# Attention beside a gated GLU on one core: the values' PSUM bank released after each run of value matmuls, queries split into two parts when they are made, and a new order of the work

## The chip, the cores and the metric

One core of one Trainium2 chip runs the whole kernel. The metric is the device time of one launch in microseconds, the median of several runs. The kernel before has a median of 1625.59 us over three runs (1625.26 to 1625.67).

## The reference

With S = 2048 rows, D = 512, H = 32 heads of width 16, one shared head of keys and values, and F = 1792, all in fp32:

```python
q = (x @ wq).reshape(B, S, H, Dh).transpose(0, 2, 1, 3)
k, v = x @ wk, x @ wv                                   # one head, width 16
p = softmax(einsum("bhqd,bkd->bhqk", q, k) * Dh ** -0.5)
a = einsum("bhqk,bkd->bhqd", p, v) -> (B, S, 512) @ wo
b = (sigmoid(x @ w_gate) * (x @ w_up)) @ w_down
g = sigmoid((x * gate_w).sum(-1, keepdims=True))
out = g * a + (1 - g) * b
```

## The kernel before

**Numbers split in two.** The matrix products that need fp32 accuracy run as products of two rounded parts. A tile is rounded to the matmul's own type (the high part), and what the rounding lost is kept as a second tile (the low part); `split` (line 706) does both, and a product takes three matmuls.

**Units of attention.** A unit is one block of 512 query rows for one group of four heads: 4 blocks times 8 groups are 32 units. The queries of a unit lie in a tile `qs` of 128 partitions by 2 by 512. Its upper and lower 64 partitions each hold, for one head parity, 16 rows of the high part, the same 16 rows again, 16 rows of the low part, and in the last two rows the negated row maxima; the key tile `ks` is stacked to match, so one matmul over 64 partitions gives a score block less its maximum. There are three `qs` tiles, used in turn.

A unit goes through these steps. `query` (line 901) makes queries of two units on TensorE, `query_out` (904) copies them out of PSUM on ScalarE, `store_q` (908) sends them to DRAM. `load_q` (919) brings them back with six DMAs into the tile `stage`, and `stack` (926) makes the parts of `qs` from it on GpSimd (a cast of the whole tile and two subtractions over 16 partitions; for unit 0 on ScalarE and VectorE). `maximum` (1062) forms scores without the maxima, 64 matmuls, each followed by a VectorE reduction that reads its PSUM bank. `max_turn` (940) transposes the maxima on TensorE, and `send_max` writes them into `qs`. `scores` (1071) forms 64 score blocks, and ScalarE's exponential takes each from PSUM into a tile `p` (22 buffers). `pv`, line 955 (the matmuls carry line 958), multiplies the exponentials of 128 keys by the values: 16 steps to a unit, each of four matmuls 32 columns wide that lie side by side on the array (eight records in the trace), all 16 adding into one PSUM bank. A column of ones beside the values gives the softmax sums. `finish` (963) copies that bank out on ScalarE, and `store`, `sums`, `invert`, `send_inverse`, `spread` and `divide` do the division.

**The GLU beside it.** `fill` (1035) issues the matmuls of gate, up, down and output projections, each on 64 of the 128 partitions. `h_split`, `w_split` and `add_part` are GpSimd's share of it.

**The order of everything.** The class `State` holds a plan of the core: clocks of each engine, when each of the 8 PSUM banks is free, when buffers and DMAs are done. The string `ORDER` is the list of TensorE's steps, found by a search beforehand, and `plan()` walks it. One character is one step. A hexadecimal digit is a step in the two halves of the array: its two upper bits say what the first 64 partitions do and the two lower bits what the other 64 do (1 a maximum, 2 a score block, 3 a GLU matmul, 0 nothing). `V` is a value step on all 128 partitions, `T` a transpose of maxima, `G` a projection of queries or keys or a turn of the values, `.` a short time in which TensorE is given nothing. All work of the other engines is placed by the plan between these steps: what depends on a step is put on its engine's queue behind it, and GpSimd's tasks are picked by rank when their inputs should be there. At the end of the program, each engine's instructions are chained in exactly this order. A wrong guess of the plan costs a wait and nothing else.

In the order before, a value step may stand anywhere; the unit's bank (`self.sum`) is taken at its first value step and given back after its 16th (`issue_v`):

```python
        if c == 0:
            self.sum = self.take()
        self.acts.append(("values", u, c, self.sum))
...
        if c == NC - 1 and u < NU - 1:
            self.acts.append(("finish", u, self.sum))
```

Of the kernel before, what the change touches and what calls it, by code (L numbers as in the profile page):

```python
# [9 lines left out]
F32 = mybir.dt.float32  # L10
# [8 lines left out]
P = 128  # L19
# [11 lines left out]
RAW, WB, DB, PB, HB, BA_BUFS = 2, 2, 4, 22, 6, 4  # L31
# [11 lines left out]
RED, GATED, SUM, ENDS, PARTS, INVERSE = 260, 258, 285, 60, 225, 70  # L43
# [67 lines left out]
class State:  # L111

    def __init__(self):
# [27 lines left out]
        self.loaded, self.stage_free, self.unit_ready, self.max_ready, self.q_ready = 0, 0, {}, {}, {}  # L141
# [52 lines left out]
    def may(self, t):  # L194
        what, u, *_ = t[3]
        if what == "h" and self.slot_of("hl") is None or what == "divide" and self.slot_of("o") is None:
            return False
        if what == "stack" and (min(self.mp) < (u - 1) * NC * 2 or min(self.ep) < (u - 2) * NC * 2):
            return False
        return t[2] <= self.now  # L200

    def run(self, t):
        self.tasks.remove(t)
        what, *args = t[3]
        if what == "w":
            wide = args[0][0] in "gu"
            cost = (not self.early(args[0])) * CAST_W + TWO_W if wide else (1 + (args[0][0] != "e")) * (CAST + TWO)
        else:
            cost = {"h": CAST + TWO, "add": TWO, "stack": CAST_W + 2 * TWO_W, "divide": CAST + 2 * TWO, "x": 2 * TWO,
                    "xf": 4 * TWO, "wq": TWO}[what]  # L210
# [13 lines left out]
        elif what == "stack":  # L224
            self.stage_free, self.unit_ready[args[0]] = at, at + SURE
# [45 lines left out]
    def event(self, what, args):  # L271
# [3 lines left out]
        elif what == "store_q":  # L275
            at = self.send(1, 256)
            self.q_ready[tuple(args)] = at
            self.ba_release(("query", *args), at)
        elif what == "stack":
            self.stage_free = self.unit_ready[args[0]] = self.on("dve", self.on("act", self.now, 2 * COPY), 4 * RED)  # L280
# [8 lines left out]
        elif what == "store":  # L289
            self.after(self.send(5, 136) + SAFE, "sums", *args)  # L290
# [164 lines left out]
    def load_next(self):  # L455
        u = self.loaded
        if u < NU and self.stage_free <= self.now and self.q_ready.get((u // NG, u % NG // 2), NEVER) <= self.now:
            self.acts.append(("load_q", u))
            self.stage_free = NEVER
            self.loaded += 1  # L460
            at = self.send(6, 384)
            if u == 0:
                self.after(at, "stack", u)
            else:
                self.task(0, at, "stack", u)
# [35 lines left out]
    def can_v(self):  # L501
        return (self.first > GROUPS.index(("turn", NB - 1, 0)) and self.vp < NU * NC and bool(self.exps)
                and (self.vp % NC > 0 or min(self.free) <= self.now)
                and self.exps[0][0] == 4 and self.exps[0][1] <= self.now)

    def issue_v(self):
        u, c = divmod(self.vp, NC)
        if c == 0:
            self.sum = self.take()
        self.acts.append(("values", u, c, self.sum))  # L510
# [5 lines left out]
        if c == NC - 1 and u < NU - 1:  # L516
            self.acts.append(("finish", u, self.sum))
            at = self.on("act", self.now + LATE, COPY) + TAIL_A
            self.free[self.sum] = at + FREE
            self.after(at, "store", u)  # L520
# [24 lines left out]
    def issue_g(self):  # L545
# [9 lines left out]
        else:  # L555
# [11 lines left out]
            else:  # L567
                at = self.on("act", at, COPY)
# [28 lines left out]
    def step(self, code):  # L597
# [10 lines left out]
        else:  # L608
            if self.full:
                self.now += OUT  # L610
# [11 lines left out]
    "GGGGGGGG555G555G5554GG5551G55G555GG5545G55G555G555GG555G555GT555Gd7fffd7bedbf7edbf7e9fe7fbde7bf9f6fedbf6fffd7bdf"  # L622
    "e7bf9f6fd7d7efVVVV96bfff9f7def6ffd7d7VVV96ffdf6ff9ff6fdbf7bdfe7fdbf6ffdb7dfef7V969V696V596VTVb9f7ff9f6ffdef6fdfb"
    "7edff6fbdf7bf9f7fed6.VV965VV96fdfb7eff96fbdf6fbdef6f9fb7edbf6fbde7fbd7eV969V696V969V696V969V696V956VVTbe9ff7ef9f"
    "e7bf9fe7ef9V695VV696Vb9fe7fedbf6fbdef6fbd7VVVdb6fbde7fbdeb7edbf7edffbf6fdbf6f9f7ebdef7VVV969V569VV697fff9f7efdef"
    "7bdV6bdeff6fbdbf6fbdef6fbdbf6VV969VT695VV6b9fff6fdebf6ff9f7df79VV6e9fff6fdbef6ff9f7d7VV96bffd7ef9fe7bde7bf9f7eed"
    "bf7f9ef6ff9f6fd7bdVVV695VV6bedff6fbdbf6fbdef6fbd7VVV9ebf7fedbf6fbdeffb5V696VT965VV95efffbf6bfdef6fbd7f9.VV6dbfef"
    "6fbd7fbde7ffdb6VVd6bfdb7ef9fe7bdef6f9fffb7efdbf6f9fe7bdef7VV969V696V596VV9eb7ff9fe7ef9fe7bf9f7d7VVVT9eeff7ef9fe7"
    "bf9fe7eV969V695VV6bdff7edbf7fedb7ff9f6ffdef6fdfb7bdf7d7dVVV79ef7edbf6f9fe7bdef6fbdb7efdb7ef9fe7bdef6fbV9a6V955VV"
    "696V9a6V969VTVV6fbdef6fbdbf6fd7df6VV9fb7fed7bfef9fe7bf9f7deV695VV6bedff6fbdbf6fd7df6VV96bffd7bf9fe7edbe7f9f7edbV"  # L630
    "V696V9e7bff9f7deV6bdfef7bd7eVV96fbff9f7ed.Ve6fdbf7bef9VTV6dbff7edbef7bf9f7edf6V965VVb9fe7fedbf6fbdef6fd7bVV96fdf"
    "f6fdbf7bfde7fd7VVd6fbdb7ef9fe7bdef6f9ffffb7edbf6f9f7ebdef7df6f9ff7d7bffdf7dfVV69aVV69aV696Va95V696VTV9eb7ff9fe7e"
    "f9fe7bf9fe7df6fbdVVV6fb9ff6fde7fbe.9.V696V965VVd6bfdb7ef9f6fdbe7bfdef6f9f7bedbf7ef9f6fd7d7VV965VVbdef6fbdbf6fbde"
    "f6fd7bVVV9ebf7fedbf6fbdef6fbdbVTV6bf9ff6fedbf6fdb7f9VVV69efff6fdb7f9ff6fedf7d7V9a6V965VV5bedfb7ef9f6fbde7bf9fffe"
    "7efd7fbedbf7edbf6..VV9651VVb6bfdfe7bf9fe7ef9fe7dVVV6bbdff6fbdefb7efdbe7dV696V969V569VTVb6fbdfe7bf9fe7ef9fe7dVV6b"
    "f9ff6fbdef6fbdf79f4dVV79fe7edbf6fbde7bf9f6ffffe9f7df6f9ff7edbfVV655VV969Ve6bfdfb7ef9fe7bf9fe7ef9f7d7VVVT9eeff7be"
    "df7bef9V696V965VV96dfff6ff9f7bfdebf7dfe7beff5f9fef7fbde7V969VVV6bdef7bdfe7bedb7ebf9f7efde7fbd6fbde7bf9f7deVV696V"
# [537 lines left out]
```

## Time and profile before

| | |
|---|---|
| median of three runs | 1625.59 us |
| span of the profiled execution, first to last instruction | 1623.6 us |
| TensorE matmul busy | 1615.1 us, 99% of the span, 12918 matmuls |
| VectorE busy | 1413.0 us, 87%, 2358 instructions |
| ScalarE busy | 1184.5 us, 73%, 2274 instructions |
| GpSimd busy | 774.2 us, 48%, 598 instructions |
| DMA | 98.09 MB, mean 60 GB/s |
| granted TensorE clock | 1.000 |

In the profile PE is TensorE's matmul and PEld its weight load, DVE is VectorE, ACT ScalarE, POOL GpSimd, SP the queue that issues the DMAs. In a timeline the first column is the start in us from the begin of the span, the second the length, and x8 the number of instructions merged into the row. A row of two matmuls on 64 partitions each that start together is one step of two halves. In a table of lines there stand the busy time, the mean ns of one instruction, and the idle time of the engine just before them with what ended it.

### The profile page before, as it was taken

What the parts mean: (1) busy time and instruction counts of PE and PEld (TensorE: products, weight loads), DVE (VectorE), ACT (ScalarE), POOL (GpSimd) and SP (SyncE); (2) the same over time, 40 slices, a digit from 0 to 9 for tenths busy, and PEclk for the clock granted to TensorE, in tenths of its full rate; (3) what the DMA queues carried; (4) which work ended last, traced back from release to release, by engine and by line L of the source; (5) the groups of instructions that cost most, each with busy time, mean ns of one, the idle gap of its engine ahead of it and who ended that gap; (6) DMA issues with size and microseconds to landing.
All of it is one profiled execution on the core that took longest, in us unless ns stands there. A gap on an engine that the chain in (4) does not pass through costs nothing.

```text
span 1623.6 us, 33417 instructions
## 1 busy us (share of the span) xinstructions
PE 1615.1 (99%) x12918; PEld 976.3 (60%) x12918; DVE 1413.0 (87%) x2358; ACT 1184.5 (73%) x2274; POOL 774.2 (48%) x598
## 2 busy tenths in 40 slices
PE   9999999999999999999999999999999999999998
PEld 7765566556566565655665556665566656565554
DVE  6999898989998998989889999988998988998842
ACT  4267777778777777777767777767877777787786
POOL 5354264356453535354735446435745453536253
PEclk9999999999999999999999999999999999999999
DMA  7411111024111212111411111102411121211011
GB/s 238 142 40 45 44 54 53 22 70 109 57 43 49 76 35 67 31 44 54 124 41 57 57 57 55 49 26 70 109 57 47 45 77 31 70 31 35 31 35 40
DMA packets 52371, 98.09 MB, mean 60 GB/s; under 512 B 17976, under 2 KB 19512, under 8 KB 51188
## 3 DMA queue, kind: packets, MB, share of 16 engines
q1 hardware_dynamic: 52212, 95.96, 19.2%
q8 instruction: 101, 1.65, 0.4%
q14 instruction: 58, 0.48, 0.1%
HBM read 74.05 MB, written 8.90 MB: 51 GB/s over the span
## 4 chain that ended last, share of the span: by engine, by line
PE 99%; ACT 0%; DVE 0%; issue 0%; DVEq 0%; POOL 0%; ACTq 0%; POOLq 0%
PE bank L1046 31%; PE bank L958 30%; PE bank L1067 18%; PE bank L1076 16%; PE bank L814 4%; PE bank L944 0%; ACT p L1078 0%; PE bank L836 0%; DVE ba L1123 0%; PE bank L884 0%; PE bank L1119 0%; ACT x L732 0%; ACT ba L1027 0%; DVE ba L1009 0%; DVEq L1171 0%
## 5 line engine op out<-in xcount | busy, mean ns | idle before, releaser
L1069 DVE TENSOR_REDUCE mx<-bank 128x1 f32<-128x512 f32 x2048 | 1285.4, 683 | 131.6 <-PE bank L1067 65.8
L1078 ACT ACTIVATE p<-bank 128x512 f32<-128x512 f32 x2048 | 1064.7, 618 | 331.7 <-PE bank L1076 171.2
L1076 PE MATMUL bank<-qs,ks 64*128 64x512 f32 x2048 | 743.5, 406 | 0.0
L1067 PE MATMUL bank<-ks,qs 62*128 62x512 f32 x2048 | 714.5, 410 | 0.5 <-ACT q L906 0.3
L958 PE MATMUL bank<-p,v_aug 128*32 128x512 f32 x4096 | 503.1, 600 | 0.0
L1076 PEld LDWEIGHTS bank<-qs,ks 64*128 64x128 f32 x2048 | 356.4, 185 | 136.7 <-DVE mx L1069 58.9
L1067 PEld LDWEIGHTS bank<-ks,qs 62*128 62x128 f32 x2048 | 343.5, 184 | 156.6 <-DVE mx L1069 55.1
L1046 PE MATMUL bank<-wd,hl 64*128 64x512 f32 x1344 | 261.8, 393 | 0.0
L958 PEld LDWEIGHTS bank<-p,v_aug 128*32 128x32 f32 x4096 | 101.8, 108 | 224.7 <-issue 199.2
L1046 PE MATMUL bank<-xs,wu 64*128 64x512 f32 x672 | 211.4, 392 | 0.0
L1046 PE MATMUL bank<-x,wu 64*128 64x512 f32 x672 | 210.1, 393 | 0.0
L1046 PE MATMUL bank<-xs,wg 64*128 64x512 f32 x672 | 210.0, 392 | 0.0
L1046 PE MATMUL bank<-x,wg 64*128 64x512 f32 x672 | 207.7, 392 | 0.0
L1046 PEld LDWEIGHTS bank<-wd,hl 64*128 64x128 f32 x1344 | 181.8, 185 | 27.6 <-issue 2.5
L932 POOL TENSOR_TENSOR qs<-stage,qs 16x1024 fp32r<-16x1024 f32 x62 | 148.7, 2398 | 4.8
L1046 PEld LDWEIGHTS bank<-x,wg 64*128 64x128 f32 x672 | 118.7, 185 | 11.2 <-POOL wu L790 0.8
L1046 PEld LDWEIGHTS bank<-x,wu 64*128 64x128 f32 x672 | 117.0, 185 | 12.0 <-issue 2.5
L1046 PEld LDWEIGHTS bank<-xs,wu 64*128 64x128 f32 x672 | 118.1, 186 | 9.2 <-issue 0.8
L1046 PEld LDWEIGHTS bank<-xs,wg 64*128 64x128 f32 x672 | 118.1, 186 | 8.8
L930 POOL CAST qs<-stage 128x1024 fp32r<-128x1024 f32 x31 | 32.3, 1041 | 158.0 <-PE bank L1076 101.2
L1030 POOL TENSOR_TENSOR ba<-ba,pa_d 128x512 f32<-128x512 f32 x48 | 61.9, 1291 | 91.8 <-DVE ba L1009 72.2
L789 POOL CAST wu<-ru 128x1024 fp32r<-128x1024 f32 x27 | 28.0, 1038 | 158.3 <-PE bank L1046 110.3
(85 smaller groups left out, 1064.4 us busy)
## 6 DMA issues: line engine op xcount, KB each, us to landing
rg<-wg SPq DMA_DIRECT2D x28, 512.0 KB
ru<-wu SPq DMA_DIRECT2D x28, 512.0 KB
rd<-wd SPq DMA_DIRECT2D x28, 512.0 KB
stage<-qd SPq DMA_DIRECT2D x192, 64.0 KB
xs<-x SPq DMA_DIRECT2D x16, 512.0 KB
xf<-x_in SPq DMA_DIRECT2D x16, 256.0 KB
qd<-q SPq DMA_DIRECT2D x16, 256.0 KB
ra<-wo SPq DMA_DIRECT2D x8, 512.0 KB
```

Source lines behind the costliest of these rows:

```text
L789: nc.gpsimd.tensor_copy(WS[item][:, 0, :], raw)
L814: nc.tensor.matmul(ps, w[:, p, part(kc)], X[b, kc][:, q, :], start=i == 0, stop=i == 3 * KC - 1)
L930: (nc.scalar.copy if u == 0 else e.tensor_copy)(qs, stage)
L932: e.tensor_tensor(qs[r], stage[r], f32(qs[r]), op=ALU.subtract)
L958: nc.tensor.matmul(ps[32 * j:32 * j + 32, :], v_aug[:, c, :], PT.pop((u, c, j)), start=c == 0, stop=c == NC - 1)
L1030: nc.gpsimd.tensor_tensor(BA[b, t], BA[b, t], PA.pop((b, t)), op=ALU.add)
L1046: nc.tensor.matmul(banks[i], l, r, start=at == 0, stop=at == j.n - 1)
L1067: nc.tensor.matmul(banks[i], qs_t[u % 3][r, pr, part(qt)], ks[r, kb * 512:(kb + 1) * 512], start=True, stop=True)
L1069: nc.vector.tensor_reduce(MX[u][:, pr, h, qt, kb:kb + 1], banks[i], axis=AX.X, op=ALU.max)
L1076: nc.tensor.matmul(banks[i], ks[r, part(c)], qs_t[u % 3][r, pr, :], start=True, stop=True)
L1078: nc.scalar.activation(p, banks[i], AF.Exp, scale=0.25)
```

## The change

Three things are changed, and the order is searched anew for them.

1. **The value bank.** A run of value steps now ends with the first two-half step behind it, or with the unit. `release` closes the accumulation there, and `finish` copies the bank out on ScalarE and gives it back. The first part of a unit goes to a tile `ou` (two buffers); each further part goes to a tile `vp` (two buffers), and `add_sums` adds it to `ou` on GpSimd. The next run takes a fresh bank. The last unit keeps one bank for all its runs.
2. **The queries.** `query_out` makes the two parts at once, ScalarE the high one and VectorE the low one, each its own `p` buffer; `store_q` sends both, two DMAs in place of one; `load_q` brings them straight into `qs`, six DMAs as before. `stack` and the tile `stage` are gone. The three `qs` tiles are zeroed once at the start, in place of `stage`.
3. **Buffers.** There are 21 `p` buffers in place of 22.

```diff
-RAW, WB, DB, PB, HB, BA_BUFS = 2, 2, 4, 22, 6, 4
+RAW, WB, DB, PB, HB, BA_BUFS = 2, 2, 4, 21, 6, 4
+OU, VB = 2, 2
...
     def issue_v(self):
         u, c = divmod(self.vp, NC)
-        if c == 0:
+        if self.sum is None:
             self.sum = self.take()
-        self.acts.append(("values", u, c, self.sum))
+        self.run_of.append(["values", u, c, not self.run_of, False, self.sum])
+        self.acts.append(self.run_of[-1])
...
+        if c == NC - 1:
+            self.release()
+
+    def release(self):
+
+        u, last = (self.vp - 1) // NC, self.vp % NC == 0
+        if u < NU - 1 or last:
+            self.run_of[-1][4] = True
+        if u == NU - 1:
+            return
+        self.run_of = []
+        if self.first_part:
...
+            self.acts.append(("finish", u, True, self.sum))
+            at = self.on("act", max(self.now + LATE, self.sums_free[i]), COPY)
...
+        else:
+            k = self.vp_free.index(min(self.vp_free))
+            assert self.vp_free[k] < NEVER
+            self.acts.append(("finish", u, False, self.sum))
+            at = self.on("act", max(self.now + LATE, self.vp_free[k]), COPY)
+            self.vp_free[k] = NEVER
+            self.task(0, at + SURE, "add_sums", u, last, k)
+        self.first_part = last
+        self.free[self.sum], self.sum = at + TAIL_A + FREE, None
...
         else:
             if self.full:
+                if self.sum is not None:
+                    self.release()
                 self.now += OUT
...
     def query_out(b, t, ps):
-        QD[b, t] = ap.tile([P, TB], F32, tag="p", name=f"q{b}_{t}", bufs=PB)
-        nc.scalar.copy(QD[b, t], ps)
+        hi, lo = QD[b, t] = [ap.tile([P, TB], F32R, tag="p", name=f"q{b}_{t}_{i}", bufs=PB) for i in range(2)]
+        nc.scalar.copy(hi, ps)
+        nc.vector.tensor_tensor(lo, ps, f32(hi), op=ALU.subtract)
...
-    def stack(u):
-
-        qs = qs_t[u % 3]
-        e = nc.vector if u == 0 else nc.gpsimd
-        (nc.scalar.copy if u == 0 else e.tensor_copy)(qs, stage)
-        for r in (slice(32, 48), slice(96, 112)):
-            e.tensor_tensor(qs[r], stage[r], f32(qs[r]), op=ALU.subtract)
+            for n, i in enumerate((0, 0, 1)):
+                r = 64 * par + n * DH
+                nc.sync.dma_start(qs[r:r + DH], qd[i, g % 2, par].rearrange("d pr t -> d (pr t)"))
...
-    def pv(u, c, ps):
+    def pv(u, c, start, stop, ps):
 
         for j in range(4):
-            nc.tensor.matmul(ps[32 * j:32 * j + 32, :], v_aug[:, c, :], PT.pop((u, c, j)),
-                             start=c == 0, stop=c == NC - 1)
...
+            nc.tensor.matmul(ps[32 * j:32 * j + 32, :], v_aug[:, c, :], PT.pop((u, c, j)), start=start, stop=stop)
...
+    def finish(u, whole, ps):
+
+        to = ap.tile([P, TB], F32, tag="ou" if whole else "vp", name=f"ou{u}", bufs=OU if whole else VB)
+        nc.scalar.copy(to, ps)
...
+    def add_sums(u, *_):
+        nc.gpsimd.tensor_tensor(SUMS[u], SUMS[u], PARTS_OF[u].pop(0), op=ALU.add)
```

`ORDER` is replaced as a whole. One line from its first tenth and its last line, before and after:

```diff
-    "bf7f9ef6ff9f6fd7bdVVV695VV6bedff6fbdbf6fbdef6fbd7VVV9ebf7fedbf6fbdeffb5V696VT965VV95efffbf6bfdef6fbd7f9.VV6dbfef"
...
-    "feVVaaVeec8V8ececV88cccccV"
+    "df6fddd7dVVVTV6ef7f6f9febdf6f9f6fbe7fbdf9e7fe7bf9dbf6ff5dVV695VV696V5bfef6f9fbdef6bdb7ff5dVV5a6.V969V7b6efdfe79f"
...
+    "Vaa8VV..............Vcccccccccccc"
```

Counted in the two strings. A stretch is what stands between two hexadecimal digits, made of `V`, `T`, `G` and `.` with at least one letter; a run holds value steps of one unit with nothing but `T` or `.` between them, and after the change each run of the units 0 to 30 is one part with a `finish` of its own.

| | before | after |
|---|---|---|
| value steps `V`, transposes `T`, projections and turns `G` | 512, 32, 24 | 512, 32, 24 |
| two-half steps, steps of one half | 4236, 28 | 4242, 16 |
| stretches, of them with a `V` | 307, 293 | 239, 224 |
| `T` with a `V` or `G` on both sides | 14 | 26 |
| runs of the units 0 to 30 | 282 | 232 |
| `.` | 10 | 23, of them 14 ahead of the last `V` |
| `c` behind the last `V` | 0 | 12 |

More of the change, by code (lines that the diff above doesn't have):

```diff
@@ L223, in run @@
             self.add_done(*args[1:], at)
-        elif what == "stack":
-            self.stage_free, self.unit_ready[args[0]] = at, at + SURE
+        elif what == "add_sums":
+            u, last, k = args
+            self.vp_free[k] = at
+            if last:
+                self.after(at, "store", u)
         elif what == "divide":
@@ L275, in event @@
         elif what == "store_q":
-            at = self.send(1, 256)
+            at = self.send(2, 512)
             self.q_ready[tuple(args)] = at
             self.ba_release(("query", *args), at)
-        elif what == "stack":
-            self.stage_free = self.unit_ready[args[0]] = self.on("dve", self.on("act", self.now, 2 * COPY), 4 * RED)
         elif what == "turn_x":
@@ L502, in can_v @@
         return (self.first > GROUPS.index(("turn", NB - 1, 0)) and self.vp < NU * NC and bool(self.exps)
-                and (self.vp % NC > 0 or min(self.free) <= self.now)
+                and (self.sum is not None or min(self.free) <= self.now)
                 and self.exps[0][0] == 4 and self.exps[0][1] <= self.now)
@@ L515, in issue_v @@
         self.vp += 1
[L516 to L520, printed above, removed]
+        if c == NC - 1:
[8 more added lines that the diff above has]
+        if self.first_part:
+            i = u % OU
+            assert self.sums_free[i] < NEVER
+            self.acts.append(("finish", u, True, self.sum))
+            at = self.on("act", max(self.now + LATE, self.sums_free[i]), COPY)
+            self.sums_free[i] = NEVER
+            if last:
+                self.after(at + TAIL_A, "store", u)
+        else:
[7 more added lines that the diff above has]
+        self.free[self.sum], self.sum = at + TAIL_A + FREE, None
     def can_t(self):
@@ L621 @@
 ORDER = (
[L622 to L626, printed above, removed]
@@ L632 @@
[L632 to L636, printed above, removed]
@@ L830, in tile_kernel @@
     nc.gpsimd.memset(v_aug, 1.0)
-    stage = cp.tile([P, 2, TB], F32, name="stage")
-    nc.gpsimd.memset(stage, 0.0)
+    qs_t = [cp.tile([P, 2, TB], F32R, name=f"qs{i}") for i in range(3)]
+    for i in range(3):
+        nc.gpsimd.memset(f32(qs_t[i]), 0.0)
     def early(n):
@@ L854, in tile_kernel @@
     gom = cp.tile([P, NC], F32, name="gom")
-    qs_t = [cp.tile([P, 2, TB], F32R, name=f"qs{i}") for i in range(3)]
     wq_s = []
```

118 lines of the change are left out of this document (62 added, 56 removed).

## The prediction

> **What bounds the kernel now.** I read the page's busy times first, then the busy times in three stretches, then the chain that ended last.
>
> ```profile
> span 1623.6 us, 33417 instructions
> PE 1615.1 (99%) x12918; PEld 976.3 (60%) x12918; DVE 1413.0 (87%) x2358; ACT 1184.5 (73%) x2274; POOL 774.2 (48%) x598
> 120.00:1600.00 1480.00, 1479.76 (x12113) 885.86 (x12107) 1304.75 (x2166) 1115.59 (x2148) 715.00 (x551) 1.00 0.18 54
> PE 99%; ACT 0%; DVE 0%; issue 0%; DVEq 0%; POOL 0%; ACTq 0%; POOLq 0%
> ```
>
> Between 120 and 1600 us TensorE lacks 0.24 us of being busy throughout, and the chain is TensorE from end to end. A busy TensorE may still be slow, though, since the rows say only that some matmul is in flight. So I look at how far apart its steps start, in a timeline of TensorE alone, ahead of and behind two runs of value steps (L958; x8 is one `V`, x24 three, x4 one cut by the window's end):
>
> ```profile
> 610.21 0.40 PE L1076 MATMUL bank<-qs,ks 64*128 64x512 f32 x1
> 610.45 0.39 PE L1046 MATMUL bank<-x,wg 64*128 64x512 f32 x1
> 610.78 1.07 PE L958 MATMUL bank<-p,v_aug 128*32 128x512 f32 x8
> 611.77 0.50 PE L1076 MATMUL bank<-qs,ks 64*128 64x512 f32 x1
> 612.12 0.63 PE L1076 MATMUL bank<-qs,ks 64*128 64x512 f32 x2
> 612.35 0.40 PE L1067 MATMUL bank<-ks,qs 62*128 62x512 f32 x1
> 612.68 2.78 PE L958 MATMUL bank<-p,v_aug 128*32 128x512 f32 x24
> 615.39 0.50 PE L1067 MATMUL bank<-ks,qs 62*128 62x512 f32 x1
> 615.74 0.39 PE L1046 MATMUL bank<-xs,wu 64*128 64x512 f32 x1
> 615.97 0.39 PE L1067 MATMUL bank<-ks,qs 62*128 62x512 f32 x1
> ```
>
> A two-half step takes 0.23 to 0.24 us (610.21 to 610.45, 615.74 to 615.97). The last one ahead of a value step takes 0.33 (610.45 to 610.78), 0.10 more. A lone value step takes 0.99 (610.78 to 611.77) and three take 2.71 (612.68 to 615.39), so a value step inside a run takes (2.71 - 0.99) / 2 = 0.86, and the last of a run 0.13 more. The first two-half step behind a run takes 0.35 (611.77 to 612.12; 615.39 to 615.74), 0.12 more. Going from two halves to the whole array and back thus costs 0.10 + 0.13 + 0.12 = 0.35 us by these rows, each good to 0.01 or 0.02. Behind the run quoted further down the first step takes 0.34 (1222.64 to 1222.98). I take 0.33 for the whole and keep 0.31 to 0.35.
>
> This makes the span up: 4236 two-half steps of 0.234 are 991 us, 512 value steps of 0.86 are 440, 307 stretches of 0.33 are 101; 92 of the 1623.6 us are left for 24 projections and turns, 32 transposes, the start and the end. Waiting adds little: in the table of waits (us in all, times, longest) the score blocks' weight loads wait for a reduction 71 times, never over 0.8 us.
>
> ```profile
> PEld bank L1076 <- DVE mx L1069: 58.9, 71, 0.8
> PEld bank L958 <- issue: 199.2, 630, 0.4
> PEld bank L958 <- ACT p L1078: 21.7, 59, 0.7
> ```
>
> (Most of these figures are the idle weight path between loads, which the matmuls cover.) So the time is the count of TensorE's steps times their durations, and a stretch fewer is worth 0.33 us, if nothing new waits.
>
> **The order.** The stretches go from 307 to 239: 68 x 0.33 = 22.4 us less. The two-half steps go up by 6 (+1.4 us), the one-half steps down by 12; of those the `c` at the end cost a full step and the others, of alternating halves, about half of one, so they give back about as much. Transposes move into the middle of runs:
>
> ```profile
> 1220.44 1.07 PE L958 MATMUL bank<-p,v_aug 128*32 128x512 f32 x8
> 1221.44 0.28 PE L944 MATMUL bank<-consts,mm 128*16 128x128 f32 x1
> 1221.64 1.06 PE L958 MATMUL bank<-p,v_aug 128*32 128x512 f32 x8
> 1222.64 0.49 PE L1076 MATMUL bank<-qs,ks 64*128 64x512 f32 x1
> 1222.98 0.40 PE L1076 MATMUL bank<-qs,ks 64*128 64x512 f32 x1
> ```
>
> The value step ahead of the transpose takes 1.00, not 0.86, and so does the one behind it, where the run ends: a `T` in the middle pays the way out of a value step once more, about 0.13. There are 26 - 14 = 12 more of them: +1.6 us. Left of the saving: 20.8 us.
>
> The Trainium skill, "TensorEngine Tiling (Array Packing)", Key Properties, says that changing the tiling mode drains TensorE. By that rule a transpose between value steps is a change on each side and would cost two drains; at a whole 0.33 us each of the 12 the saving would be 18.4 us. The rows show only the one 0.13, and the sum goes by them.
>
> **The fresh bank of each run.** After the change each of 232 runs opens a bank that an exponential or a reduction has just left, where now 31 units do. The weight loads of value steps that waited for an exponential idled 21.7 / 59 = 0.37 us each, those that waited for nothing visible 199.2 / 630 = 0.32. The difference, 0.05, times 201 more openings is 10 us; but the bank is also one more to choose from, so below it the bound is nothing. The timeline gives a nearer price: the first and the last of the 31 openings that follow a two-half step are
>
> ```profile
> 92.43 0.39 PE L1046 MATMUL bank<-x,wu 64*128 64x512 f32 x1
> 92.77 0.64 PE L958 MATMUL bank<-p,v_aug 128*32 128x512 f32 x4
> 1535.73 0.39 PE L1046 MATMUL bank<-xs,wu 64*128 64x512 f32 x1
> 1536.06 1.06 PE L958 MATMUL bank<-p,v_aug 128*32 128x512 f32 x8
> ```
>
> and all 31 start 0.359 us behind the step ahead on the average, the 262 other run starts 0.341. I take the 0.018 between them, 3.6 us.
>
> **ScalarE's copies, GpSimd's sums, the queries.** These lie beside TensorE.
>
> ```profile
> L966 ACT COPY ou<-bank 128x512 f32<-128x512 f32 x31 | 18.3, 591 | 40.2 <-PE bank L958 40.2
> L1078 ACT ACTIVATE p<-bank 128x512 f32<-128x512 f32 x2048 | 1064.7, 618 | 331.7 <-PE bank L1076 171.2 <-PE bank L1067 120.6 <-PE bank L1046 31.6
> L1030 POOL TENSOR_TENSOR ba<-ba,pa_d 128x512 f32<-128x512 f32 x48 | 61.9, 1291 | 91.8 <-DVE ba L1009 72.2 <-ACT pa_d L1027 12.0 <-ACT p L1078 3.8
> L932 POOL TENSOR_TENSOR qs<-stage,qs 16x1024 fp32r<-16x1024 f32 x62 | 148.7, 2398 | 4.8
> L930 POOL CAST qs<-stage 128x1024 fp32r<-128x1024 f32 x31 | 32.3, 1041 | 158.0 <-PE bank L1076 101.2 <-PE bank L1067 51.1 <-PE bank L1046 5.7
> L738 POOL TENSOR_TENSOR x<-xf,x 128x512 fp32r<-128x512 f32 x8 | 10.1, 1292 | 12.0 <-ACT x L732 12.0
> L738 DVE TENSOR_TENSOR x<-xf,x 128x512 fp32r<-128x512 f32 x8 | 6.5, 847 | 4.3 <-ACT x L732 4.3
> L877 DVE SCALAR_TENSOR_TENSOR ks<-kh,consts,bank 128x512 fp32r<-128x512 f32 x4 | 3.0, 748 | 3.2 <-ACT kh L876 3.0
> ```
>
> ScalarE gets 232 - 31 = 201 copies of 0.59 us, 119 us: from 1184.5 to 1303, 81% of about 1607. The 331.7 us that it idles ahead of exponentials covers them. Behind each copy are queued the exponentials of the next score blocks, for whose `p` the next run waits; the copy delays them by 0.59 us, which the 21 buffered `p` (five value steps) hide. Without that cover a run would start up to 0.59 later.
>
> GpSimd loses 148.7 + 32.3 = 181 us of stacking and gets 201 additions of 1.29 us, 259 us, and two more zeroings: 774 to some 855 us, 53%. Behind an addition are queued the splits of weights and hidden rows; for the addition itself waits the `vp` buffer, for that the second next `finish`, and behind that on ScalarE all exponentials. I cost this at nothing while the two buffers hold; the rival below prices it.
>
> The Trainium skill, "GPSIMD Engine Reference", 4.1 Engine selection, speaks against this choice: a two-input elementwise operation belongs on VectorE, GpSimd being about half as fast. Here the same 128x512 subtraction takes 1292 ns on one and 847 on the other, a factor of 1.5. By the rule the 201 additions would go to VectorE, and at 847 ns they would bring its 1423 us (below) to 1593, 99% of the new span, and it would then be the bound; by the rows GpSimd has the room.
>
> VectorE gets 16 subtractions out of PSUM. The nearest row is 748 ns: +12 us, all in the first 100 us, less two of unit 0's stack; 1423 us, 89%. Bounds: nothing, if they fall beside the projections (12 matmuls, some 2.8 us of TensorE, for each), to 10 us, if the first maxima wait for them; I take nothing, since VectorE was busy for 44 of the first 60 us.
>
> ```profile
> 0.00:60.00 60.00, 58.35 (x268) 43.17 (x269) 44.03 (x78) 26.48 (x43) 34.06 (x27) 1.00 0.71 224
> qd<-q SPq DMA_DIRECT2D x16, 256.0 KB
> stage<-qd SPq DMA_DIRECT2D x192, 64.0 KB
> ```
>
> The queue SP gets 16 more stores of 256 KB, 4.2 MB; at the 224 GB/s of these 60 us that is 19 us of transfer, in a stretch where the engines are 71% busy. Only unit 0 waits for its own, and loses its stack (a 1.05 us cast and two subtractions); I cost it at nothing, with 2 us either way. For all later units the load is issued about when the stack ran before, and the 1.04 + 2 x 2.40 us of stacking fall away ahead of the first maximum; TensorE did not wait there, so this gains nothing.
>
> **The end.** Fourteen `.` stand ahead of the last value step and the last 12 GLU matmuls behind it.
>
> ```profile
> 1611.32 1.31 PE L1046 MATMUL bank<-we,o 64*128 64x512 f32 x5
> 1612.56 1.06 PE L958 MATMUL bank<-p,v_aug 128*32 128x512 f32 x8
> 1614.12 0.71 PE L1105 MATMUL bank<-consts,ou_last 128*128 128x128 f32 x4 [0.49 <-ACT ou_last L1103]
> ```
>
> A one-half step costs 0.23 here ((1.31 - 0.39) / 4 for five). Twelve take 2.8 us behind the last value step, in which the copy hides that TensorE waits for now (0.49); before, ten of them stood ahead of it. The wait for the last exponentials and the additions behind the 12 cost between 0 and 2 us; I take 1.
>
> **The sum.** -20.8 + 3.6 + 1 = -16.2 us. The profiled span is 1623.6, so 1607.4; the median lies 2.0 us above the span, and I forecast **1609.4 us**. This case alone runs from 1601 (68 x 0.35, nothing for the banks and the end, 2 gained at the start) to 1621 (68 x 0.31, 10 lost at the banks, 2 at the end, some 3 at the start).
>
> **Rivals.** *The additions hold ScalarE up (slower).* Place: a unit's third and later parts. GpSimd works off its queue in order; a wide split is 1.04 + 2.39 us, two hidden rows 2 x 1.9. If it is in such work while two parts wait, the next `finish` has no `vp` buffer, ScalarE stands with the exponentials behind it, and TensorE stops at the next run. With runs 3 us apart, as between the short stretches, and 7.2 + 1.3 us ahead of the first free buffer, one such event costs some 2.5 us. Eight would bring the gain under 0.2%, twelve would give 1639 us. For it: GpSimd is at 53% and ScalarE has only this ring of two. Against it: the additions have first rank, and the waits quoted show that TensorE hardly ever stood for a task placed by the order. 8%.
>
> *ScalarE's copies eat the gain.* Its exponentials are late by part of each copy: 0.09 us in each of 201 parts costs 18 us, giving 1625 to 1628. For it: 81% busy and idle during long runs, so the rest must suffice. Against it: 300 us idle are left. 7%.
>
> *The stretches are not what costs.* If the 0.33 us is not paid for the change between forms but for something which stands at those places, say the weights' first load, it still stands there 68 times less. If it is a wait for exponentials, it moves into the longer runs and the time stays at 1622 to 1626. The nearly equal 0.33 and 0.35 at each run speak against a wait. 4%.
>
> **How the numbers follow.** The forecast's case has 81%. The range 1601 to 1622 holds it and the near edge of the two middle rivals. A measurement of this kernel can tell about 0.2% (3.3 us) from no change: faster has the 81% and a few points of the middle rivals, 0.85; no change 0.06; slower 0.09.
>
> **What would show it.** In the profile after: TensorE's steps still 0.234 us apart, 0.86 inside a run, 0.33 for each of 239 stretches; copies of value sums 232, additions 201 at 1.29 us; ScalarE about 1303 us, GpSimd 855, VectorE 1423; no waits of the value steps' weight loads above 1 us. It would be wrong if ScalarE's copies wait for GpSimd's additions, if gaps of 1 us and more appear ahead of runs, or if a run's first value step starts 0.05 us and more later than now.

## The result and the profile after

| | before | after |
|---|---|---|
| median of four runs | 1625.55 us (1625.26 to 1625.67) | 1600.24 us (1598.83 to 1600.78) |
| span of the profiled execution | 1623.6 us | 1597.1 us (that execution: 1598.83 us) |

The ratio is 0.9842, 95% interval 0.9828 to 0.9856. The change makes the kernel 25.3 us faster; 16.2 were predicted.

First, lines of the page of the kernel after: the busy times, the chain that ended last, and three groups of instructions.

```profile
PE 1587.9 (99%) x12918; PEld 998.6 (63%) x12918; DVE 1392.0 (87%) x2372; ACT 1258.4 (79%) x2474; POOL 848.0 (53%) x708
PE 98%; ACT 0%; DVE 0%; DMA 0%; POOL 0%; issue 0%; DVEq 0%
L984 ACT COPY ou<-bank 128x512 f32<-128x512 f32 x232 | 140.9, 608 | 266.6 <-PE bank L977 122.2
L991 POOL TENSOR_TENSOR ou<-ou,ou 128x512 f32<-128x512 f32 x201 | 259.0, 1289 | 204.9 <-ACT ou L984 199.2
L1103 ACT ACTIVATE p<-bank 128x512 f32<-128x512 f32 x2048 | 1050.1, 652 | 2.6 <-PE bank L1101 0.4
```

TensorE makes the same 12918 matmuls and is still nearly the whole chain (98%), busy for 27.2 us less. The copies and additions are there in the numbers that were foretold (232 and 201), and an addition has the price foretold (1289 ns). The copies wait for TensorE first of all (122.2 us). So the time has to be looked for in how far apart TensorE's steps start. In the timeline of TensorE at the end of a run of three value steps (the window cuts off the first of them):

```profile
799.81 1.90 PE L977 MATMUL bank<-p,v_aug 128*32 128x512 f32 x16
801.64 0.50 PE L1092 MATMUL bank<-ks,qs 62*128 62x512 f32 x1
801.98 0.39 PE L1101 MATMUL bank<-qs,ks 64*128 64x512 f32 x1
802.21 0.39 PE L1071 MATMUL bank<-xs,wg 64*128 64x512 f32 x1
```

The last two value steps of the run take 1.83 us, the first step behind them 0.34, the next one 0.23: the prices of before, within 0.02. Summed over all starts of both timelines (a step starts with its first record and lasts until the next step on TensorE starts):

| | before | after | worth in the span |
|---|---|---|---|
| steps and changes between the two forms, by their counts at before's mean durations | | | -20.4 us |
| a two-half step ahead of another one, mean | 233.9 ns (3636) | 232.2 ns (3770) | -6.2 us |
| the last two-half step ahead of a value step, mean | 343.8 ns (285) | 342.9 ns (217) | about 0 |
| a value step ahead of a value step, mean | 877 ns | 878 ns | 0 |
| the end | | | about +0.2 us |
| sum; the spans differ by | | | -26.4; -26.5 us |

Part of the 6.2 us stands in single long steps. Of these two-half steps 38 take over 260 ns before, 4.27 us above the median together; after it are 13, 0.73 us. That is 3.5 us. Not all of it is waiting that the released bank could end: 1.5 us of before's 4.27 belong to three steps ahead of steps of one half. One stands at 38.5 us, where a maximum waits for the copy of a query; two stand at 1608 us, where one half of the array works off steps of one half and the other has none. What is left is 2.7 us in 35 steps before, so waits account for 2.0 us of the gain. The other 2.7 us are 0.7 ns on each of 3770 steps; the section on the new order without the released bank comes back to them.

### The profile page after: what moved, and what is told of

Same layout as the page of the kernel before. It is cut to its first block, busy times and chain, and to the rows that moved or that the text cites. A ratio compares the mean times of both kernels' runs of the same rounds, so it can differ in the third digit from the quotient of the medians.

```text
span 1597.1 us, 33902 instructions
## 1 busy us (share of the span) xinstructions
PE 1587.9 (99%) x12918; PEld 998.6 (63%) x12918; DVE 1392.0 (87%) x2372; ACT 1258.4 (79%) x2474; POOL 848.0 (53%) x708
## 3 DMA queue, kind: packets, MB, share of 16 engines
q8 instruction: 101, 1.65, 0.4%
## 4 chain that ended last, share of the span: by engine, by line
PE 98%; ACT 0%; DVE 0%; DMA 0%; POOL 0%; issue 0%; DVEq 0%
PE bank L1071 31%; PE bank L977 29%; PE bank L1092 18%; PE bank L1101 16%; PE bank L838 4%; ACT p L1103 0%; PE bank L963 0%; PE bank L908 0%; DVE ba L1148 0%; DVE ba L1034 0%; DMA wkv_raw<-wkv 0%; POOL wkv_s L732 0%; DVE wkv_stack L869 0%; PE bank L1144 0%; DVEq L1196 0%
## 5 line engine op out<-in xcount | busy, mean ns | idle before, releaser
L1094 DVE TENSOR_REDUCE mx<-bank 128x1 f32<-128x512 f32 x2048 | 1257.4, 681 | 133.8 <-PE bank L1092 80.5
L1103 ACT ACTIVATE p<-bank 128x512 f32<-128x512 f32 x2048 | 1050.1, 652 | 2.6 <-PE bank L1101 0.4
L1101 PE MATMUL bank<-qs,ks 64*128 64x512 f32 x2048 | 698.0, 400 | 0.0
L1092 PE MATMUL bank<-ks,qs 62*128 62x512 f32 x2048 | 686.6, 406 | 0.0
L977 PE MATMUL bank<-p,v_aug 128*32 128x512 f32 x4096 | 491.3, 598 | 0.7 <-ACT p L1103 0.7
L991 POOL TENSOR_TENSOR ou<-ou,ou 128x512 f32<-128x512 f32 x201 | 259.0, 1289 | 204.9 <-ACT ou L984 199.2
L984 ACT COPY ou<-bank 128x512 f32<-128x512 f32 x232 | 140.9, 608 | 266.6 <-PE bank L977 122.2
L977 PEld LDWEIGHTS bank<-p,v_aug 128*32 128x32 f32 x4096 | 107.7, 109 | 232.2 <-issue 188.1
L1071 PEld LDWEIGHTS bank<-wd,hl 64*128 64x128 f32 x1344 | 195.0, 185 | 20.4 <-ACT p L1103 1.7
L1071 PE MATMUL bank<-x,wu 64*128 64x512 f32 x672 | 194.5, 391 | 0.0
L1071 PE MATMUL bank<-x,wg 64*128 64x512 f32 x672 | 190.4, 391 | 0.0
```

The costliest lines, as they stand in the source:

```text
L977: nc.tensor.matmul(ps[32 * j:32 * j + 32, :], v_aug[:, c, :], PT.pop((u, c, j)), start=start, stop=stop)
L984: nc.scalar.copy(to, ps)
L991: nc.gpsimd.tensor_tensor(SUMS[u], SUMS[u], PARTS_OF[u].pop(0), op=ALU.add)
L1071: nc.tensor.matmul(banks[i], l, r, start=at == 0, stop=at == j.n - 1)
L1092: nc.tensor.matmul(banks[i], qs_t[u % 3][r, pr, part(qt)], ks[r, kb * 512:(kb + 1) * 512], start=True, stop=True)
L1094: nc.vector.tensor_reduce(MX[u][:, pr, h, qt, kb:kb + 1], banks[i], axis=AX.X, op=ALU.max)
```

## Experiments

Ten kernels were run, each timed against the kernel before on the same chip (its medians there: 1625.55 to 1626.13 us).

| kernel | median us | ratio to before, 95% interval | span us |
|---|---|---|---|
| before | 1625.55 | 1 | 1623.6 |
| before, 68 more stretches | 1650.33 | 1.0151 (1.0135 to 1.0166) | 1648.8 |
| before, with the split queries | 1638.34 | 1.0077 (1.0062 to 1.0092) | 1636.7 |
| the same, with the bank released | 1659.07 | 1.0201 (1.0186 to 1.0216) | 1656.6 |
| after's plan on the old order, queries only | 1758.49 | 1.0811 (1.0793 to 1.0829) | 1761.2 |
| after's plan on the old order, bank released | 1829.90 | 1.1255 (1.1238 to 1.1272) | 1826.5 |
| **after** | **1600.24** | 0.9842 (0.9828 to 0.9856) | 1597.1 |
| after, one bank kept for a unit | 1674.46 | 1.0302 (1.0287 to 1.0318) | 1674.4 |
| after, additions on VectorE | 1696.12 | 1.0432 (1.0414 to 1.0449) | 1694.3 |
| after, additions twice | 1610.85 | 0.9909 (0.9894 to 0.9924) | 1609.2 |
| after, one `vp` buffer | 1712.60 | 1.0528 (1.0510 to 1.0545) | 1713.3 |
| after, another end | 1600.09 | 0.9842 (0.9828 to 0.9857) | 1596.5 |

The theory on trial is the prediction's: each change of form costs TensorE a third of a microsecond, the new order makes 68 fewer, and the rest is hidden. The rivals: the stretches are not what costs; ScalarE and GpSimd are near to taking the gain; the gain comes from the queries or from the released bank in itself. The third part of the change, 21 `p` buffers in place of 22, was not tried by itself.

### The price of a stretch

In the kernel before, 68 runs of two value steps are broken: the second one goes behind the next two-half step. Nothing else is changed. For example, in `ORDER`:

```diff
-    "f6fbdef6fbd7f9VV6fb9ff6fedbf6fdf6f9VV697V..."
+    "f6fbdef6fbd7f9V6Vfb9ff6fedbf6fdf6f9V6V97V..."
```

> The kernel before with 68 of its runs of two value steps broken up: the second value step is put one two-half step later, so there are 375 stretches in place of 307 and no other difference. By the price of a stretch, 0.31 to 0.35 us, it takes 1647 to 1649 us. If the surplus at the edges of a run is waiting, which would be spent anyway, it takes 1626 to 1635.

The span is 25.2 us longer, 25.2 / 68 = 0.37 us for each. In the timeline of TensorE of this kernel, at one broken pair:

```profile
611.80 1.07 PE L958 MATMUL bank<-p,v_aug 128*32 128x512 f32 x8
612.79 0.49 PE L1076 MATMUL bank<-qs,ks 64*128 64x512 f32 x1
613.22 1.06 PE L958 MATMUL bank<-p,v_aug 128*32 128x512 f32 x8
614.22 0.49 PE L1067 MATMUL bank<-ks,qs 62*128 62x512 f32 x1
```

The two-half step between the value steps takes 0.43 us (612.79 to 613.22), 0.20 more than its 0.23: it pays the way out of one form and the way into the other, and the value steps ahead of it and behind it (0.99 and 1.00) pay for the ends of their runs. No row names a wait. Of the 25.2 us, 1.4 are not this price: there are 50 two-half steps above 260 ns in place of 38. The rest is 0.35 us for each, within the 0.31 to 0.35 that I had read off three places, and the rival "the stretches are not what costs" falls.

### The parts of the change without the new order

The first attempt took after's code and put before's order in it, once with the bank kept for a unit and once with it released:

```diff
-RAW, WB, DB, PB, HB, BA_BUFS = 2, 2, 4, 21, 6, 4
-OU, VB = 2, 2
+RAW, WB, DB, PB, HB, BA_BUFS = 2, 2, 4, 22, 6, 4
+OU, VB = 2, 1
...
-                if self.sum is not None:
-                    self.release()
```

(the last two lines go in the first kernel only; `ORDER` is that of before in both.)

> The old order and one value bank for a whole unit, with the new query path (split when made, loaded as parts, no stack on GpSimd). If TensorE's steps are all that counts, and if what was gained beyond the stretches comes from the bank, this takes 1624 to 1627 us, as before. If the stacks on GpSimd were what held TensorE up, it takes about 1619 us, with two-half steps shorter by 1.6 ns on the average.

> The old order (307 stretches) with all the rest of the change: the value bank given back behind each of 282 runs, 251 additions on GpSimd, the new queries; one vp buffer in place of two, and 22 p buffers, since the old order needs them. Theory of the stretches alone: 1624 to 1627, since their number is as before. Theory that the bank given back takes away waits of the two-half steps: 1618 to 1621, with fewer waits of weight loads for reductions. If the copies and additions cost TensorE something in themselves: above 1628.

They took 1758.49 and 1829.90 us, some 130 and 200 us above the kernel before, and they tell nothing of the parts. After's plan expects other times than those that the old order was made for; walked with that order it places most side work wrongly, and it even issues the first three score blocks of unit 0 ahead of the sending of its maxima, so that these are computed without them. The lesson is in the method: an order that was searched for one plan need not be fit for another. So the parts were built anew on before's own plan, order and buffers.

In the first of these the six loads bring the parts straight into `qs`, at the place where `stack` stood, and `store_q` sends the two parts:

```diff
-        QD[b, t] = ap.tile([P, TB], F32, tag="p", name=f"q{b}_{t}", bufs=PB)
-        nc.scalar.copy(QD[b, t], ps)
+        hi, lo = QD[b, t] = [ap.tile([P, TB], F32R, tag="p", name=f"q{b}_{t}_{i}", bufs=PB) for i in range(2)]
+        nc.scalar.copy(hi, ps)
+        nc.vector.tensor_tensor(lo, ps, f32(hi), op=ALU.subtract)
...
     def stack(u):
...
+                nc.sync.dma_start(qs[r:r + DH], qd[i, g % 2, par].rearrange("d pr t -> d (pr t)"))
```

> The kernel before with its own order, plan, buffers and value banks, and only the queries changed: split when made, two stores, and the six loads straight into the unit's tile where the stack on GpSimd stood. If the stacks lay beside TensorE's work, 1624 to 1627 us as before, with GpSimd some 180 us less busy. If GpSimd's time or the way of a unit's queries held TensorE up, 1618 to 1622.

It is 13.1 us slower by the span, which neither expectation had. Its page has GpSimd at 180 us less, and this gains nothing:

```profile
PE 1622.0 (99%) x12918; PEld 985.7 (60%) x12918; DVE 1420.3 (87%) x2372; ACT 1183.7 (72%) x2273; POOL 594.5 (36%) x507
```

The starts of its steps fall behind before's by 13.4 us up to before's step at 81 us, and the difference stays between 13.3 and 13.9 from there to the end. So all of it lies in the start. The rows of the stretches 0 to 30 and 30 to 90 us (after the length: PE busy, PEld, DVE, ACT, POOL, clock, DMA share, GB/s), of this kernel and then of before and after:

```profile
0.00:30.00 30.00, 24.73 (x108) 20.32 (x108) 14.20 (x24) 15.48 (x26) 12.35 (x15) 0.99 0.73 244
30.00:90.00 60.00, 56.93 (x242) 38.52 (x243) 53.47 (x100) 12.48 (x21) 12.41 (x9) 0.95 0.59 188
```

```profile
0.00:30.00 30.00, 28.61 (x130) 22.58 (x132) 15.95 (x27) 16.70 (x28) 10.95 (x14) 1.00 0.73 244
30.00:90.00 60.00, 59.74 (x328) 43.17 (x326) 57.34 (x106) 22.32 (x42) 25.43 (x16) 1.00 0.45 135
```

```profile
0.00:30.00 30.00, 27.66 (x126) 22.31 (x127) 18.48 (x32) 13.29 (x22) 10.13 (x13) 1.00 0.66 218
30.00:90.00 60.00, 60.00 (x329) 43.70 (x329) 57.12 (x107) 21.32 (x39) 18.23 (x12) 1.00 0.68 221
```

With before's order TensorE is idle for 8.3 of the first 90 us (before: 1.65). It makes 350 matmuls there; after makes 455, nearly as many as before with its 458, and is idle for 2.3 us.

The largest loss is the first maximum step, which waits for unit 0's parts. The loads for unit 0 in the queue SP, of before and then of this kernel, and the steps of TensorE here:

```profile
15.58 2.65 SPq L924 DMA_DIRECT2D stage<-qd  x6
24.13 4.14 SPq L933 DMA_DIRECT2D qs<-qd  x6
31.31 2.08 PE L1068 MATMUL bank<-ks,qs 62*128 62x512 f32 x6 [4.89 <-DMA qs<-qd]
33.31 4.42 PE L817 MATMUL bank<-x,wq 128*128 128x512 f32 x12
```

The loads stand where `stack` stood, 8.5 us later than before's, and TensorE waits 4.89 us. Around this wait, from 29.5 to 36.3 us, the granted clock is 0.50 (hence the 0.95 above), and 12 matmuls of a projection take 4.42 us in place of 3.0. Together 7.5 of the 13 us are lost by the end of these two rows. This points to the place of the loads in this variant more than to the split queries: after, with split queries, issues its loads from 18.4 us on and starts its first maximum at 23.7 us without such a wait. A variant of before with earlier loads was not run. The other losses, up to 0.9 us each, are places where a projection and a maximum step follow each other; one maximum there waits 0.95 us for VectorE's subtraction. That the new order is what hides this price, by spreading the projections, is argued from these rows and not tried by itself.

The second one also releases the bank behind each of the old order's 282 runs, with 251 additions, two `vp` buffers and one `ou`:

```diff
-        if c == 0:
+        if self.sum is None:
             self.sum = self.take()
...
+                if self.sum is not None:
+                    self.release()
```

> The old order with the queries changed as in queries_alone, and the value bank given back behind each of its 282 runs (251 additions on GpSimd; one ou buffer, two vp buffers). The stretches are 307 as before. If the bank given back takes waits from the two-half steps and nothing else changes, 1618 to 1623 us. If the stretches are all, 1624 to 1627. If 251 more copies on ScalarE and the additions cost TensorE something in an order that was not laid out for them, above 1628.

It is 19.9 us slower again by the span (1656.6 against 1636.7), 1.6 us of it in the start and the rest spread over the whole in steps of 0.3 to 0.8 us; 89 two-half steps take over 260 ns, 16.8 us (with the split queries alone 49, 6.9 us), and the step ahead of a run takes 369 ns on the average (346). ScalarE's waits ahead of its copies of value sums (us in all, times, longest):

```profile
ACT ou L1001 <- PE bank L994: 162.0, 113, 3.5
ACT ou L1001 <- POOL ou L1008: 38.7, 22, 4.0
```

The ring that the first rival described is at work here: 22 times the copy stands for an addition. So the released bank by itself gains nothing in the time. In an order that wasn't laid for its copies and additions it costs.

### The new order without the released bank

After, but with one bank for a unit's 16 value steps, 31 copies and no additions (the plan's assertions on free times are loosened as well, here and in the kernels that leave its timing):

```diff
-                if self.sum is not None:
-                    self.release()
```

> The new order with one value bank for a whole unit, so with 31 copies, no additions, and seven banks for all other work. Theory that the new order is what gains, by its 239 stretches: 1600 to 1603. Theory that the order needs the bank that is given back: two-half steps wait for banks, 1606 us or more; each wait for a reduction or an exponential costs 0.1 to 1 us.

It is 77.3 us above after in the span. The loss grows evenly, some 2 us in each 38. In the timeline of TensorE of this kernel, at one place, and at the same steps of after:

```profile
900.84 0.65 PE L1090 MATMUL bank<-ks,qs 62*128 62x512 f32 x2
901.49 0.49 PE L1099 MATMUL bank<-qs,ks 64*128 64x512 f32 x1
901.82 0.39 PE L1069 MATMUL bank<-xs,wu 64*128 64x512 f32 x1
```

```profile
860.46 0.42 PE L1092 MATMUL bank<-ks,qs 62*128 62x512 f32 x2
860.70 0.39 PE L1101 MATMUL bank<-qs,ks 64*128 64x512 f32 x1
860.93 0.39 PE L1071 MATMUL bank<-xs,wu 64*128 64x512 f32 x1
```

The step that starts at 900.84 takes 0.65 instead of 0.24, and the one behind it 0.33 instead of 0.23. Score blocks and maxima have one bank fewer to go to, and stand for the exponential or the reduction that is still reading the next one. There are 593 such steps above 260 ns (after: 13), worth 56.2 us, and the step ahead of a run takes 403 ns. The table of waits says what for (first this kernel, then after):

```profile
PEld bank L1090 <- DVE mx L1092: 47.4, 106, 0.8
PEld bank L1090 <- ACT p L1101: 47.0, 182, 0.8
```

```profile
PEld bank L1092 <- DVE mx L1094: 15.7, 22, 0.8
PEld bank L1092 <- ACT p L1103: 30.1, 47, 0.8
```

The new order can be followed at this speed only because the bank comes back. A released bank is not a price paid at each opening, as my sum had it, but what keeps 593 steps from waiting.

The steps that show no wait differ too. The means of the two-half steps of at most 260 ns (behind a two-half step and ahead of one):

| kernel | bank kept | bank released |
|---|---|---|
| before; before, 68 more stretches | 232.7; 232.6 ns | |
| before's order with the split queries | 232.4 ns | 232.1 ns |
| the new order | 233.5 ns | 232.1 ns |
| the new order, another end; additions twice | | 232.0; 232.1 ns |

Kernels that should agree do so within 0.1 ns. The released bank takes off 0.4 ns in the old order and 1.4 in the new one, the split queries 0.3. So the 0.7 ns from before to after come without the new order: 0.3 with the split queries and 0.4 with the released bank. That they are waits too short to stand out is likely, but no row shows it.

### The engine for the additions

```diff
-        nc.gpsimd.tensor_tensor(SUMS[u], SUMS[u], PARTS_OF[u].pop(0), op=ALU.add)
+        nc.vector.tensor_tensor(SUMS[u], SUMS[u], PARTS_OF[u].pop(0), op=ALU.add)
```

> The kernel after with the 201 additions on VectorE in place of GpSimd. At the 847 ns that VectorE took for a 128x512 subtraction they add 170 us to its 1392, which makes 1562, or 98% of the span. If VectorE then sets the pace, its reductions give banks back later and TensorE waits: 1610 to 1640 us. If it has the room, 1599 to 1602.

97.2 us above after in the span, 1696 us where 1610 to 1640 were expected. The page, then the group of the additions (shortest, median and longest ns), then two rows of the table of waits:

```profile
PE 1650.9 (97%) x12918; PEld 994.2 (59%) x12918; DVE 1535.6 (91%) x2573; ACT 1289.5 (76%) x2474; POOL 610.7 (36%) x507
```

```profile
L991 DVE TENSOR_TENSOR ou<-ou,ou x201: 627/681/2862, 114.9 to 1650.7; 128x512 f32<-128x512 f32 x101
```

```profile
PEld bank L1101 <- DVE mx L1094: 88.2, 162, 2.6
PEld bank L1092 <- DVE mx L1094: 49.5, 105, 1.7
```

An addition takes 681 ns at the median here and 1289 on GpSimd, and still the kernel is slower. VectorE is at 91%, not the 99% that I had worked out with 847 ns, and not the bound by its busy time. It is the engine whose reductions give the PSUM banks back, and behind an addition they come later: the weight loads of score blocks and of maxima wait 162 and 105 times for a reduction, up to 2.6 us (score blocks in before, in the row that the prediction quotes: 71 times, up to 0.8). 440 two-half steps exceed 260 ns, 82.6 us. The Trainium skill, "GPSIMD Engine Reference", 4.1 Engine selection, puts elementwise work of two inputs on VectorE. Its reason holds here, a factor of 1.9; what it would make of the time doesn't, by 97 us, with plan and order left as they are. An order searched for additions on VectorE was not tried.

### How near GpSimd and ScalarE are to taking the gain

Two kernels load the ring of the rival. One makes every addition twice:

```diff
-        nc.gpsimd.tensor_tensor(SUMS[u], SUMS[u], PARTS_OF[u].pop(0), op=ALU.add)
+        to = PARTS_OF[u].pop(0)
+        nc.gpsimd.tensor_tensor(SUMS[u], SUMS[u], to, op=ALU.add)
+        nc.gpsimd.tensor_tensor(SUMS[u], SUMS[u], to, op=ALU.add)
```

> The kernel after with each of the 201 additions issued twice on GpSimd (so each further part counts twice in the sums). GpSimd gets 259 us more, some 1107, 69%. If GpSimd's additions are near to holding up ScalarE's copies and through them TensorE, above 1606 us; if they lie beside everything, 1599 to 1602.

GpSimd goes from 848.0 to 1105.6 us (69%), and the span grows by 12.1 us. 9.5 us of this lie at five places, 0.9 to 3.5 us at each. One of them, in the timelines of ScalarE and of GpSimd:

```profile
299.56 0.58 ACT L984 COPY ou<-bank 128x512 f32<-128x512 f32 x1 [2.80 <-POOL ou L993]
298.26 1.27 POOL L993 TENSOR_TENSOR ou<-ou,ou 128x512 f32<-128x512 f32 x1
```

The copy waits 2.80 us until the additions (the second one ends at 299.53) have freed a `vp` buffer. In the timeline of TensorE, this place and two others:

```profile
300.20 0.50 PE L1103 MATMUL bank<-qs,ks 64*128 64x512 f32 x1 [1.25 <-ACT ou L984]
766.99 0.50 PE L1103 MATMUL bank<-qs,ks 64*128 64x512 f32 x1 [1.45 <-ACT pa_d L1054]
1152.24 0.50 PE L1073 MATMUL bank<-wd,hl 64*128 64x512 f32 x1 [0.84 <-POOL wd L732]
```

TensorE stands for ScalarE 1.25 us at the first one. This is the ring of the rival, at some half of the price that it put on an event (2.5 us). The second is of the same kind, by way of another of GpSimd's additions. The third is another one: the weights of the down projection are split too late, and TensorE waits for GpSimd itself. Of the two places that are not shown, one is like the third and one is a wait for a reduction. It takes 201 additions more to bring about these five places, and two of them are the ring's.

The other takes one of the two `vp` buffers away (the `p` buffer comes back, 22):

```diff
-RAW, WB, DB, PB, HB, BA_BUFS = 2, 2, 4, 21, 6, 4
-OU, VB = 2, 2
+RAW, WB, DB, PB, HB, BA_BUFS = 2, 2, 4, 22, 6, 4
+OU, VB = 2, 1
```

> The kernel after with one vp buffer in place of two (and 22 p buffers). Each further part's copy on ScalarE must then wait until GpSimd has added the one before it. If ScalarE has enough finished exponentials ahead of TensorE, 1599 to 1603 us. If the ring between ScalarE and GpSimd is what would hold TensorE up, as in the rival of the prediction, 1606 us or more, with ScalarE waiting for GpSimd well over the 42 us in all that it does in the kernel after.

116.2 us above after. Waits of ScalarE ahead of its copies, in this kernel and then in after:

```profile
ACT ou L986 <- PE bank L979: 158.1, 89, 7.7
ACT ou L986 <- POOL ou L993: 65.0, 34, 5.4
```

```profile
ACT ou L984 <- PE bank L977: 122.2, 75, 5.1
ACT ou L984 <- POOL ou L991: 12.2, 12, 1.5
```

And one of the 34 in the timeline:

```profile
928.70 0.59 ACT L986 COPY ou<-bank 128x512 f32<-128x512 f32 x1 [0.71 <-issue]
929.37 1.28 POOL L993 TENSOR_TENSOR ou<-ou,ou 128x512 f32<-128x512 f32 x1 [5.69 <-ACT ou L986]
931.46 0.59 ACT L986 COPY ou<-bank 128x512 f32<-128x512 f32 x1 [1.18 <-POOL ou L993]
932.04 1.58 ACT L1105 ACTIVATE p<-bank 128x512 f32<-128x512 f32 x3
```

Behind the second copy the exponentials stand, and behind these TensorE: 359 two-half steps above 260 ns, 92.3 us. That is more than the 65 us that ScalarE waited for additions. A part of it is the clock. The mean granted clock of this execution is 0.982: in eight stretches ahead of its end, 58 us in all, it is 0.50. The longest of them as a row of its own, and two steps in the timeline of TensorE there:

```profile
1130.32:1147.39 17.07, 15.58 (x63) 7.42 (x66) 7.21 (x11) 5.40 (x10) 3.40 (x2) 0.50 0.09 27
1131.97 0.62 PE L1073 MATMUL bank<-x,wg 64*128 64x512 f32 x1
1132.40 0.62 PE L1073 MATMUL bank<-x,wg 64*128 64x512 f32 x1
```

The step from 1131.97 to 1132.40 takes 0.43 us without a wait. 69 of the 359 long steps, 23.6 of the 92.3 us, lie in these stretches, and the halved clock can account for at most 29 of the 116 us. The rest is waiting; that each late exponential also holds a bank is likely, and not shown. The slow rival was thus one buffer away. With two, after's copies wait for additions 12 times, 12.2 us (61.4 us with the waits put down to other work of GpSimd, of which the expectation's 42 are the four largest rows), and TensorE, with 0.73 us above 260 ns in all, has next to nothing of it.

### The end

```diff
-    "Vaa8VV..............Vcccccccccccc"
+    "Vaa8ccccccccVVVcccc"
```

> The kernel after with its last steps in another order: 8 of the last 12 GLU steps stand ahead of the last three value steps, and these are one run. TensorE waited 0.70 us for the last exponentials and had 2.8 us of GLU steps behind the last value step. If the end is a chain of TensorE's steps as all the rest, it gains the 0.70 us and one stretch, in all 0.5 to 1.2 us: 1599.0 to 1599.8. If the exponentials' chain on ScalarE sets the end, nothing.

1600.09 us against 1600.24 in the medians, which is no difference; the spans are 1596.5 and 1597.1. The two ends in the timeline of TensorE, after and then this kernel:

```profile
1583.80 1.06 PE L977 MATMUL bank<-p,v_aug 128*32 128x512 f32 x8 [0.70 <-ACT p L1103]
1584.79 3.03 PE L1071 MATMUL bank<-we,o 64*128 64x512 f32 x12
```

```profile
1581.46 1.98 PE L1071 MATMUL bank<-we,o 64*128 64x512 f32 x8
1583.37 2.78 PE L977 MATMUL bank<-p,v_aug 128*32 128x512 f32 x24
```

After waits 0.70 us for the last exponentials, and eight of the one-half steps put ahead of the last values fill this wait. The spans differ by 0.6 us, less than executions of one kernel do (1598.83 to 1600.78), so that the wait's worth can't be told from nothing.

## Why the prediction came out 9 us too high

The direction and the place were right: the change is worth what TensorE saves in changes of form, and the other engines' work is hidden. The median lies just below the range that I gave (1601), so the sizes failed, and by these terms:

- **The stretches: right.** -20.8 us predicted with the 12 transposes, -20.4 by the counts at the measured durations, and 0.35 to 0.37 us for each of 68 when they are put back into before.
- **The fresh bank at each opening: wrong in kind.** I put +3.6 us on 201 openings, from a difference of 0.018 us between two groups of before. The steps ahead of runs take 342.9 ns in after against 343.8, so the term is nothing. The two groups differed by where they stood, not by whether the bank was fresh: in before's order with the bank released every run opens a fresh one, and the step ahead of a unit's first run still takes longer than that ahead of the others (medians 353 and 333 ns; in before 345 and 331).
- **"Waiting adds little": wrong, the largest miss.** I left the two-half steps at before's 0.234 us. They got shorter by 6.2 us in all: 2.0 in waits, 1.5 at the three places in the start and the end, 2.7 in the steps without a visible wait. A part of the term was there to be found: 38 steps of before exceed 260 ns, and a change that gives a bank back could take most of those away. I had written that the bank "is also one more to choose from" and yet set the lower end of that cost at nothing. That the bank has to do with the long waits is shown in one direction only: without it the new order has 593 of them, while with it the old order has more (89) than without it (49). How the 2.0 us divide between bank and order stays open. The 0.7 ns of each step come without the new order, 0.3 with the queries and 0.4 with the bank.
- **The end: +1 predicted, about +0.2 measured.** The last value step waits 0.70 us, but nothing behind the 12 GLU steps was late.
- **What was costed at nothing** came out at nothing in sum: ScalarE's copies, GpSimd's additions, the queries. They cost nothing only because they were covered: it is 116 us without the second `vp` buffer, up to 29 of them by the clock, and 13 us for the queries in before's order, 7.5 of them at late loads. ScalarE came to 1258.4 us and not to 1303: the records of instructions that follow each other overlap (2048 exponentials of 652 ns would be 1335 us and fill 1050.1), so that adding whole lengths was too much. GpSimd came to 848.0 (855 predicted), VectorE to 1392.0 (1423), where the reductions overlap more as well (2048 of 683 ns filled 1285.4 us before, 2048 of 681 fill 1257.4 after).
- **The median above the span:** 3.1 us instead of 2.0, 1.1 back. The profiled execution is the fastest of the four, 1.4 us below the median.

Together -3.6 - 0.8 - 6.2 + 0.4 = -10.2 us in the span, where 10.3 are missing, and +1.1 above it.

Of the rivals, "the additions hold ScalarE up" is a mechanism that exists and has next to no effect at two buffers; "ScalarE's copies eat the gain" didn't happen, TensorE's steps ahead of runs being no longer than before; "the stretches are not what costs" is refuted. The first one's arithmetic was off: eight events of 2.5 us are 20 us, more than the whole gain of 16.2, and five would have brought it to about 0.2%. One sign of being wrong was set too sharp: copies do wait for additions, 12 times, and TensorE has next to nothing of it.

## What to carry to other kernels

Where one engine is busy throughout, read the distance of its steps' starts and not its share: here 0.33 us stood at each change of form, in rows that all say busy. A change of several parts may gain only as a whole: in the old order the queries cost 13 us (7.5 of them at that variant's late loads) and the released bank 20 more, the new order without the bank is 49 us over before, and all together save 25; so cost each part's cover, and ask what the order was laid for. Look at the granted clock of every variant before its loss is put down to waits. And before an elementwise operation goes to the engine that does it faster, look at who waits behind it there.

## What was not expected of the hardware

- A long wait on TensorE costs more than its length: the two-half step behind a step that waited took 0.33 us instead of 0.23 (901.49 to 901.82), the same 0.10 as at a change of form. In that kernel all 38 two-half steps of over 400 ns with two-half steps around them are followed by one of 0.33 us or so, but of the 363 between 300 and 400 ns only 80 by one of over 0.30.
- One of eight PSUM banks, held open between runs, costs 77 us on 1597 in this order, with 201 copies and additions saved.
- With one `vp` buffer the granted clock fell to 0.50 in eight stretches, 58 us in all, in a kernel whose TensorE is busy for 98% of the span. A two-half step took 0.43 us there.
- Two-half steps without a visible wait are 0.4 ns shorter with the bank released than with it kept in the old order, and 1.4 ns in the new one. No run says how.
